# A decode step of attention and feed-forward: wo in one ring buffer, w1 and w2 in another, w2 by block-diagonal columns of h

## The chip, the cores and the metric

The kernel runs on one core of a Trainium2 chip. The metric is the device time of one execution in microseconds (us), median over several runs; lower is better. The engines are named as the profile names them: PE is TensorE's matmuls, PEld its weight loads, DVE is VectorE, ACT ScalarE, SP the engine that issues the loads. "PEclk" is the granted TensorE clock as a share of full speed. A difference counts as faster or slower from 2% on.

## The reference

One token of 512 numbers passes a conditioned layernorm, attention of 32 query heads in 8 groups over 32768 cached positions, an output projection `wo`, a second conditioned layernorm, and a feed-forward of width 1792 with ReLU. Cut to what matters:

```python
h = _layernorm(x) * (1 + ca) + sa
x = x + ga * _A_ref(h, k_cache, v_cache, wq, wo)   # k_cache, v_cache: (1, 8, 32768, 128)
h = _layernorm(x) * (1 + cb) + sb
x = x + gb * (jnp.maximum(h @ w1, 0) @ w2)         # w1: (512, 1792), w2: (1792, 512)
return x                                           # (1, 1, 512), bfloat16
```

The K and V caches are 134 of the 149 MB that have to be read. Everything is used once.

## The kernel before

All large inputs pass through a ring of four buffers of 4 MB in one order on one queue. A transfer is issued when its buffer is free. The end of that order, and the pieces of wo and w2 (cut):

```python
WOP = [(0, Hkv // 2), (Hkv // 2, Hkv // 4), (3 * Hkv // 4, Hkv // 4)]
W2P = [(0, FA - 3), (FA - 3, 2), (FA - 1, 1)]
...
stream += [("v", LAST, (0, 1)), ("v", LAST, (2,)), ("wo", 0), ("v", LAST, (3,)), ("wo", 1), ("wo", 2)]
stream += [("w1",)] + [("w2", i) for i in range(len(W2P))]
```

Each of these ten takes a whole buffer of the ring, so most wait until an earlier one has been used up. The last quarter of V of the last head group (`LAST`) is not multiplied like the others, with 512 columns of V moving, but with V as the stationary operand and 4 columns moving, straight into the transposed output `oT_ps`:

```python
def pv(g, us, js=range(16)):
    ...
    if g == LAST and us[0] == NTILE - 1:
        for j in range(TK):                                   # 64
            c0 = REP * (4 + j // 16)
            nc.tensor.matmul(oT_ps, lhsT=Vs[0][:, j, :], rhs=PT_g[:, j % 16, c0:c0 + REP], start=False, ...)
        return
    ...
            for j in js:                                      # 16 for each quarter
                step(u, V, PTf[:, c0:c0 + 16], V[:, :, Dh * j:Dh * (j + 1)])
```

w2 is applied with one column of h as the stationary operand; the four quarters of the 512 outputs go to partitions 0, 32, 64 and 96, that is to four column groups of the array:

```python
for i in range(KT):                                           # 4
    nc.tensor.matmul(
        ffn_ps[32 * i:32 * i + 1, :], lhsT=hidT[:, ft:ft + 1],
        rhs=w2_sb[:, a, b, i * P:(i + 1) * P], start=False, stop=(ft == FT - 1), skip_group_check=True)
...
nc.scalar.dma_start(out=out[0, 0].rearrange("(i n) -> i n", i=KT),
                    in_=o_bf[:].rearrange("(i r) n -> i r n", r=32)[:, 0, :])
```

Of the kernel before, what the change touches and what calls it, by code (L numbers as in the profile page):

```python
# [9 lines left out]
BF16 = mybir.dt.bfloat16  # L10
F32 = mybir.dt.float32
# [6 lines left out]
def kernel(  # L18
# [28 lines left out]
    WOP = [(0, Hkv // 2), (Hkv // 2, Hkv // 4), (3 * Hkv // 4, Hkv // 4)]  # L47
# [4 lines left out]
    W2P = [(0, FA - 3), (FA - 3, 2), (FA - 1, 1)]  # L52
# [35 lines left out]

    def load(key):
        kind = key[0]  # L90
        if kind == "wm":
            t = ring.tile([P, KT, 6 * D], BF16, tag="slot", name="wm_sb")
            src = wm_v
        elif kind == "wq":
            t = ring.tile([P, KT, Hq * Dh], BF16, tag="slot", name="wq_sb")
            src = wq_v
        elif kind in "kv":
            g, steps = key[1], key[2]
            t = ring.tile([P, TK * len(steps), Dh], BF16, tag="slot", name="Ksb" if kind == "k" else "Vsb")
            src = (kv if kind == "k" else vv)[g, :, TK * steps[0]:TK * (steps[-1] + 1), :]  # L100
        elif kind == "wo":
            t = ring.tile([P, WOP[key[1]][1] * REP, D], BF16, tag="slot", name="wo_sb")
            src = wo_v(key[1])
        elif kind == "w1":
            t = ring.tile([P, KT, Dff], BF16, tag="slot", name="w1_sb")
            src = w1_v
        else:
            a0, n = W2P[key[1]]
            t = ring.tile([P, n, FB, D], BF16, tag="slot", name="w2_sb")
            src = w2_v[:, a0:a0 + n]  # L110
        stream_dma(t[:], src)
        if kind in "kv":
            for i, u in enumerate(steps):
                loaded[(kind, g, u)] = t[:, TK * i:TK * (i + 1), :]
        else:
            loaded[key] = t[:]
# [13 lines left out]
    stream += [("v", LAST, (0, 1)), ("v", LAST, (2,)), ("wo", 0), ("v", LAST, (3,)), ("wo", 1), ("wo", 2)]  # L130
    stream += [("w1",)] + [("w2", i) for i in range(len(W2P))]
# [38 lines left out]
    for n in sorted({n * REP for _, n in WOP}):  # L170
# [20 lines left out]

    rowsel = const.tile([P, 4], F32)
    nc.vector.tensor_copy(out=rowsel[:], in_=ident_f[:].rearrange("p (j c) -> p j c", c=32)[:, :, 0])
# [4 lines left out]
    rowpick = const.tile([P, P], F32)  # L198
    nc.gpsimd.memset(rowpick[:], 0.0)
    nc.vector.tensor_reduce(  # L200
        out=rowpick[:].rearrange("p (j m) -> p j m", m=32)[:, :, 0],
        in_=ident_f[:].rearrange("p (j m) -> p j m", m=32), op=ALU.add, axis=AX.X,
    )
    rowsum = const.tile([P, 1], F32)
    nc.vector.reduce_sum(out=rowsum[:], in_=rowsel[:], axis=AX.X)

# [35 lines left out]
    def layernorm_T(src_T, stat_in, dst_T, shiftT, nscaleT, tagp):  # L242
# [7 lines left out]
        m = nc.tensor.matmul(stat_ps[:], lhsT=onesD_f[:], rhs=stat_in[:], start=True, stop=True)  # L250
        tc.stamp_issue_order_token(m.ins, "pe_tail")
# [10 lines left out]
        a = nc.scalar.activation(out=std[:], in_=negvar[:], func=ACT.Sqrt, bias=eps_t[:], scale=-1.0)  # L262
        tc.stamp_issue_order_token(a.ins, "act_tail")
# [51 lines left out]
    def rows32(src_T, name):  # L315


        e = const.tile([P, 32, KT], F32, name=f"{name}_exp")
        nc.vector.tensor_tensor(
            out=e[:], in0=src_T.unsqueeze(1).to_broadcast([P, 32, KT]),  # L320
            in1=place32[:].unsqueeze(2).to_broadcast([P, 32, KT]), op=ALU.mult,
        )
        r_ps = bank(f"{name}_ps")[:, 0:P]
        m = nc.tensor.matmul(
            r_ps, lhsT=rowpick[:], rhs=e[:].rearrange("p m kt -> p (m kt)"), start=True, stop=True,
        )
        tc.stamp_issue_order_token(m.ins, "pe_tail")
        rows = const.tile([P, P], F32, name=f"{name}_rows")
        a = nc.scalar.copy(out=rows[:], in_=r_ps)
        tc.stamp_issue_order_token(a.ins, "act_tail")  # L330
        return rows

    gb_rows = rows32(modT_sb[:, 5 * KT:6 * KT], "gb")
# [139 lines left out]
    def pv(g, us, js=range(16)):  # L473
# [4 lines left out]
        if g == LAST and us[0] == NTILE - 1:  # L478

            for j in range(TK):  # L480
                c0 = REP * (4 + j // 16)
                nc.tensor.matmul(  # L482
                    oT_ps, lhsT=Vs[0][:, j, :], rhs=PT_g[:, j % 16, c0:c0 + REP],
                    start=False, stop=(j == TK - 1), skip_group_check=True,
                )
            return
# [27 lines left out]
    def blocks(g):  # L514

        o = o_tiles.pop(g)[:].rearrange("p (s d) -> p s d", s=4)
        Y = spool.tile([16, Dh], F32, tag="Y", name="Y", bufs=1)
        nc.vector.tensor_scalar(out=Y[:], in0=o[:, 0], scalar1=smask[:, 0:1], scalar2=None, op0=ALU.mult)
        for s in range(1, 4):
            nc.vector.scalar_tensor_tensor(  # L520
                out=Y[:], in0=o[:, s], scalar=smask[:, s:s + 1], in1=Y[:], op0=ALU.mult, op1=ALU.add,
            )
        Y_tiles[g] = Y
        if g == LAST:
            nc.vector.memset(oT_ps, 0.0)

    def o_cols(g):
        nc.tensor.matmul(  # L528
            oT_ps, lhsT=Y_tiles.pop(g)[:], rhs=qsel, start=(g < LAST), stop=(g < LAST), skip_group_check=True,
        )  # L530
# [33 lines left out]
    def project(i):  # L564
# [3 lines left out]
        for r in range(n):  # L568
            if i == 0:
                nc.tensor.matmul(  # L570
                    a_rows[0][32 * (r % 4):32 * (r % 4) + 1, :], lhsT=o2_tiles[i][:, r:r + 1],
                    rhs=wo_sb[:, r, :], start=False, stop=(r >= n - 4), skip_group_check=True,
                )
                continue
# [10 lines left out]
    def join_rows():  # L585
        a_sb = rows_sb("a_sb")[:, 0, :]
        nc.scalar.copy(out=a_sb, in_=a_rows[0])
        for ko in range(KT):
            yield
            nc.tensor.matmul(  # L590
                attnT_ps[:, ko:ko + 1], lhsT=a_sb.rearrange("q (m ko) -> q ko m", ko=KT)[:, ko, :],
                rhs=rowsum[:], start=False, stop=False, skip_group_check=True,
            )

    with tc.manual_schedule(engines={mybir.EngineType.PE, mybir.EngineType.DVE}):
# [66 lines left out]
        pv(LAST, (2,))  # L662
        blocks(LAST)
        project(0)
        o_cols(LAST)
        join = join_rows()
        next(join)
        pv(LAST, (3,))
        next(join)
        next(join)  # L670
        normalise(LAST)
        for _ in join:
            pass
        for i in range(1, len(WOP)):
            project(i)


    ffn_ps = bank("ffn_ps")[:, 0:P]
    nc.vector.memset(ffn_ps, 0.0)
    stat2 = const.tile([P, 2], F32)  # L680
    x1T = const.tile([P, KT], F32)
    nc.vector.tensor_tensor(out=x1T[:], in0=attnT_ps, in1=modT_sb[:, 2 * KT:3 * KT], op=ALU.mult)
    nc.vector.scalar_tensor_tensor(
        out=x1T[:], in0=x1T[:], scalar=1.0, in1=xT, op0=ALU.mult, op1=ALU.add, accum_out=stat2[:, 0:1],
    )
    h2T = const.tile([P, KT], BF16)
    layernorm_T(x1T[:], stat2, h2T[:], modT_sb[:, 3 * KT:4 * KT], ncb[:], "ln2")

    x1_rows = rows32(x1T[:], "x1")

    w1_sb = need(("w1",))
    w1_f = w1_sb.rearrange("p kt (a m b) -> p kt a b m", m=P, b=FB)
    hidT_ps = small_ps([P, FT], "hidT_ps")
    for ft in range(FT):
        for kt in range(KT):
            nc.tensor.matmul(
                hidT_ps[:, ft:ft + 1], lhsT=w1_f[:, kt, ft // FB, ft % FB, :], rhs=h2T[:, kt:kt + 1],
                start=(kt == 0), stop=(kt == KT - 1),
            )
    hidT = const.tile([P, FT], BF16)  # L700
    nc.scalar.activation(out=hidT[:], in_=hidT_ps[:], func=ACT.Relu)
    for part, (base, n) in enumerate(W2P):
        w2_sb = need(("w2", part))
        for a in range(n):
            for b in range(FB):
                ft = (base + a) * FB + b
                for i in range(KT):
                    nc.tensor.matmul(  # L708
                        ffn_ps[32 * i:32 * i + 1, :], lhsT=hidT[:, ft:ft + 1],
                        rhs=w2_sb[:, a, b, i * P:(i + 1) * P], start=False, stop=(ft == FT - 1),  # L710
                        skip_group_check=True,
                    )
    o_rows = const.tile([P, P], F32)
    nc.vector.tensor_tensor(out=o_rows[:], in0=ffn_ps, in1=gb_rows[:], op=ALU.mult)  # L714
    o_bf = const.tile([P, P], BF16)
    nc.vector.tensor_tensor(out=o_bf[:], in0=o_rows[:], in1=x1_rows[:], op=ALU.add)  # L716
    nc.scalar.dma_start(
        out=out[0, 0].rearrange("(i n) -> i n", i=KT),
        in_=o_bf[:].rearrange("(i r) n -> i r n", r=32)[:, 0, :],
    )  # L720
# [30 lines left out]
```

## Time and profile before

356.12 us is the median of 6 runs (355.97 to 356.60).

| | before |
|---|---|
| span of the profiled run | 354.3 us |
| busy share PE, DVE, ACT | 78%, 58%, 8% |
| share of the load queue's packets | 98.2% |
| last K tile landed | 302.89 us |
| last quarter of V landed | 336.83 us |
| x1T (the input of the second layernorm) begins | 343.40 us |
| w2's matmuls | 348.6 to 350.9 us |

The busy shares say little, since the stages differ. The end is what decides: which of the last waits is for a transfer, and which for an engine. The prediction shows those views. Two more lines serve for comparison, from the views of single tiles of the kernel before; the three numbers after the colon are the shortest, median and longest duration in ns, then come first and last start:

```profile
L708 PE MATMUL ffn_ps<-w_sb,hidT x56: 264/311/315, 348.6 to 350.6; 128*1 128x128 bf16 x56
L717 ACTq DMA_DIRECT2D out_dram<-o_bf x1: 1098/1098/1098, 351.6 to 351.6; - x1
```

A single w2 matmul lasts 311 ns, yet 56 of them start within 2 us, with two waits for data among them: they overlap. The issue of the 1 KB output takes 1.1 us.

### The profile page before, as it was taken

How to read it: one execution, taken by the hardware profiler on the slowest of the kernel's cores; microseconds unless marked ns; L12 is line 12 of the kernel's file. 1: busy time of each engine (PE TensorE's matmuls, PEld its weight loads, DVE VectorE, ACT ScalarE, POOL GpSimd, SP SyncE). 2: the span in 40 equal slices, each digit the busy share in tenths (PEclk: the TensorE clock that was granted, in tenths of full speed). 3: DMA queues.
4: the chain of work that ended last, by engine and by line, in shares of the span. 5: the costliest groups of instructions: out<-in, count | busy, mean ns of one | idle time of the engine just before them, and what ended most of it. 6: DMA issues, size and time to landing. Idle time of an engine off the chain costs nothing. (4 is left out here: it accounts for less than half of the span.)

```text
span 354.3 us, 4169 instructions
## 1 busy us (share of the span) xinstructions
PE 276.4 (78%) x1403; PEld 114.0 (32%) x1403; DVE 205.8 (58%) x266; ACT 28.9 (8%) x70; POOL 8.4 (2%) x14
## 2 busy tenths in 40 slices
PE   0453793799798979897979796989789787989884
PEld 0121231233233323332333233333333233333373
DVE  8537683973848366571949177553938095843221
ACT  1023004000110011001100101010100010010110
POOL 9000000000000000000000000000000000000000
PEclk9966867699899999999999998899999999999955
DMA  8999999999999999999999999999999999999994
GB/s 313 449 422 455 420 426 451 422 429 425 446 429 414 459 425 416 459 422 422 455 422 425 442 433 426 436 436 422 425 451 425 422 453 425 422 455 403 424 418 164
DMA packets 6613, 149.61 MB, mean 422 GB/s; under 512 B 712, under 2 KB 712, under 8 KB 1608
## 3 DMA queue, kind: packets, MB, share of 16 engines
q1 hardware_dynamic: 6592, 149.43, 98.2%
q8 instruction: 9, 0.15, 0.1%
q14 instruction: 4, 0.03, 0.0%
q10 hardware_dynamic: 8, 0.00, 0.0%
HBM read 149.42 MB, written 0.00 MB: 422 GB/s over the span
## 5 line engine op out<-in xcount | busy, mean ns | idle before, releaser
L398 DVE STREAM_TRANSPOSE KTt<-Ksb 128x2048 f32<-128x2048 f32 x64 | 143.3, 2283 | 61.9 <-DMA Ksb<-in_A_k_cache_dram 52.6
L489 PE MATMUL o_ps<-Vsb,PT_g 128*16 (+1 forms) x496 | 124.9, 387 | 23.4 <-ACT qbd L382 7.8
L418 PE MATMUL S_ps<-KTt,qbd 128*128 128x512 bf16 x512 | 124.1, 395 | 17.9 <-DVE KTt L398 16.2
L418 PEld LDWEIGHTS <-qbd 128*128 128x128 bf16 x512 | 50.0, 100 | 83.3 <-issue 27.4
L489 PEld LDWEIGHTS o_ps<-Vsb,PT_g 128*16 x416 | 36.4, 87 | 90.9 <-issue 66.4
L424 DVE TENSOR_SCALAR_CACHE_REDUCE S_g<-S_ps 128x512 f32<-128x512 f32 x16 | 11.1, 691 | 29.2 <-PE S_ps L418 29.2
L382 ACT COPY qbd<-qrep_sb 32x128 bf16<-32x128 bf16 x32 | 9.4, 295 | 137.1 <-PE S_ps L418 136.0
L461 DVE STREAM_TRANSPOSE PT_g<-P_g 128x1024 bf16<-128x1024 bf16 x8 | 9.7, 1218 | 6.5 <-ACT P_g L455 6.5
L452 ACT ACTIVATE nbias<-Mb_ps 128x1 f32<-128x1 f32 x8 | 1.4, 171 | 130.8 <-PE Mb_ps L450 130.8
L489 PEld LDWEIGHTS <-PT_g 128*16 128x16 bf16 x80 | 6.9, 90 | 10.1 <-issue 0.8
L219 PE MATMUL xc_ps<-cx_sel,cx_bd 16*128 16x2 bf16 x4 | 0.3, 172 | 12.1 <-DVE cx_bd L213 12.1
L455 ACT ACTIVATE P_g<-S_g,nbias 128x1024 bf16<-128x1024 f32 x8 | 9.2, 1149 | 0.2
L520 DVE SCALAR_TENSOR_TENSOR Y<-o_ps,smask,Y 16x128 f32<-16x128 f32 x24 | 8.0, 335 | 0.8
L159 DVE COPY sel<-ident_bf 128x128 bf16<-128x128 bf16 x4 | 7.5, 3688 | 0.0
L541 DVE TENSOR_TENSOR oT_sb<-acc_ps,Linv 128x4 bf16<-128x4 f32 x8 | 1.2, 151 | 9.4 <-PE acc_ps L528 5.6
L467 PE MATMUL L_ps<-Lexp,ones_f 128*128 128x4 f32 x16 | 3.0, 258 | 4.3 <-DVE Lexp L464 4.3
L439 DVE TENSOR_REDUCE Mrow<-mT_ps 1x4 f32<-1x128 f32 x8 | 2.1, 257 | 6.9 <-PE mT_ps L436 6.9
L355 PE MATMUL q_ps<-wq_sb,hT 128*1 128x512 bf16 x32 | 3.6, 625 | 3.0 <-DVE hT L270 3.0
L436 PE MATMUL mT_ps<-ident_f,m_p 128*1 128x128 f32 x8 | 2.2, 270 | 3.9 <-DVE m_p L433 2.0
L467 PEld LDWEIGHTS L_ps<-Lexp,ones_f 128*128 128x128 f32 x16 | 3.1, 222 | 5.7 <-issue 5.1
L287 PE MATMUL mod_ps<-wm_sb,siluT 128*1 128x512 bf16 x24 | 3.4, 612 | 1.2 <-DVE siluT L281 1.2
L510 DVE MEMSET o_ps<- 16x512 f32 x8 | 3.9, 485 | 0.8
(115 smaller groups left out, 84.4 us busy)
## 6 DMA issues: line engine op xcount, KB each, us to landing
Ksb<-in_A_k_cache_dram SPq DMA_DIRECT2D x16, 4096.0 KB, 29.8
Vsb<-in_A_v_cache_dram SPq DMA_DIRECT2D x15, 4096.0 KB, 24.2
wq_sb<-in_A_wq_dram SPq DMA_DIRECT2D x1, 4096.0 KB, 18.7
Vsb<-in_A_v_cache_dram SPq DMA_DIRECT2D x2, 2048.0 KB, 17.9
wm_sb<-in_w_mod_dram SPq DMA_DIRECT2D x1, 3072.0 KB, 10.3
wo_sb<-in_A_wo_dram SPq DMA_DIRECT2D x1, 2048.0 KB
wo_sb<-in_A_wo_dram SPq DMA_DIRECT2D x2, 1024.0 KB, 8.0
w_sb<-in_B_w_dram SPq DMA_DIRECT2D x1, 1792.0 KB, 10.7
```

Of the source, the lines that this page charges most:

```text
L159: nc.vector.tensor_copy(out=sel[:, hp, :].rearrange("p (a c) -> p a c", a=4), in_=src)
L355: nc.tensor.matmul(q_ps[i][32 * a:32 * a + 1, :].rearrange("o (h e) -> o h e", e=32), lhsT=hT[:, kt:kt + 1], rhs=wq_f[:, kt, i, a], start= ...
L382: nc.scalar.copy(out=o, in_=i)
L398: t = nc.vector.transpose(out=KTt[:].bitcast(F32), in_=Ksb[:, 32 * half:32 * half + 32, :].rearrange("p j d -> p (j d)").bitcast(F32),)
L418: nc.tensor.matmul(S_ps_tiles[g], lhsT=qbd[g % 2][:, hp, s, :], rhs=KTv[:, 16 * sl:16 * sl + 16, h, :, par], start=(t4 == 0 and sl == 0 an ...
L424: nc.vector.tensor_scalar(out=S_tiles[g][:, G, :], in0=S_ps_tiles[g], scalar1=1.0, scalar2=None, op0=ALU.mult, op1=ALU.max, accum_out=m_ti ...
L455: nc.scalar.activation(out=P_g[:], in_=S_g[:].rearrange("p g f -> p (g f)"), func=ACT.Exp, bias=nbias[:], scale=scale, accum_out=l_g[:],)
L461: nc.vector.transpose(out=PT_g[:], in_=P_g[:])
L467: nc.tensor.matmul(L_ps[:], lhsT=ones_f[:], rhs=Lexp[:], start=True, stop=True)
L489: nc.tensor.matmul(o_tiles[g][:], lhsT=PT, rhs=Vx, start=False, stop=False, skip_group_check=True)
L510: nc.vector.memset(o_tiles[g][:], 0.0)
L520: nc.vector.scalar_tensor_tensor(out=Y[:], in0=o[:, s], scalar=smask[:, s:s + 1], in1=Y[:], op0=ALU.mult, op1=ALU.add,)
```

## The change

The intent: with the last two quarters of V in one buffer, all of wo in a second and w1 with w2 in a third, every load can be issued early. V then comes ahead of wo, and fewer bytes and less work stand behind the last landing. The rows of wo's product are turned by VectorE instead of being picked out by matmuls of full width; for that, `project` reads the rows of wo and writes their product in another order (`"p (a m ko) -> p a ko m"`, not in the cut). Spare matmuls are put in to hold the clock; w2 accumulates into four adjacent partitions, so that the last two VectorE instructions and the output touch 4 partitions. Cut to the core:

```diff
-    WOP = [(0, Hkv // 2), (Hkv // 2, Hkv // 4), (3 * Hkv // 4, Hkv // 4)]
+    WOP = [(0, Hkv // 2), (Hkv // 2, Hkv // 4), (Hkv - 2, 1), (Hkv - 1, 1)]
-    W2P = [(0, FA - 3), (FA - 3, 2), (FA - 1, 1)]
+    W2P = [(0, 2, slice(0, FB)), (2, FA - 5, slice(0, FB)), (FA - 3, 1, slice(0, FB)), (FA - 2, 1, slice(0, FB)),
+           (FA - 1, 1, slice(0, 1)), (FA - 1, 1, slice(1, FB))]
+    W1P = [(0, KT - 1), (KT - 1, KT)]
...
+    def piece(name, at, n):
+        if name not in pieces:
+            pieces[name] = ring.tile([P, 2 * TK * Dh], BF16, tag="slot", name=name)
+        return pieces[name][:, at:at + n]
...
-    stream += [("v", LAST, (0, 1)), ("v", LAST, (2,)), ("wo", 0), ("v", LAST, (3,)), ("wo", 1), ("wo", 2)]
+    stream += [("v", LAST, (0, 1)), ("v", LAST, (2,)), ("v", LAST, (3,))] + [("wo", i) for i in range(len(WOP))]
...
-        if g == LAST and us[0] == NTILE - 1:          # the 64 small matmuls
-            ...
-            return
...
     def join_rows():
-        a_sb = rows_sb("a_sb")[:, 0, :]
-        nc.scalar.copy(out=a_sb, in_=a_rows[0])
+        aT = rows_sb("aT")[:, 0, :]
+        nc.vector.transpose(out=aT, in_=a_rows[0])
...
+    def keep_clock(n):
+        for _ in range(n):
+            nc.tensor.matmul(spare[0], lhsT=ident_bf[:], rhs=qbd[0][:, 0, 0:4, :], start=True, stop=True)
...
         pv(LAST, (2,))
+        pv(LAST, (3,))
         blocks(LAST)
         project(0)
+        keep_clock(2)
         o_cols(LAST)
+        keep_clock(2)
         normalise(LAST)
+        project(1)
+        keep_clock(3)
+        project(2)
+        join_rows()
+        keep_clock(4)
+        project(3)
...                                                    # 4 before and 4 after the layernorm statistics,
...                                                    # 1 after each of two rows of w1, 1 after w1
-                        ffn_ps[32 * i:32 * i + 1, :], lhsT=hidT[:, ft:ft + 1],
+                        ffn_ps, lhsT=hid_bd[:, ft, i, :],      # 4 columns, h in the i-th, zeros in the others
...
-        in_=o_bf[:].rearrange("(i r) n -> i r n", r=32)[:, 0, :],
+    nc.scalar.dma_start(out=out[0, 0].rearrange("(i n) -> i n", i=KT), in_=o_bf[:])
```

More of the change, by code (lines that the diff above doesn't have):

```diff
@@ L45 @@
     NG = NTILE // 2
-    WOP = [(0, Hkv // 2), (Hkv // 2, Hkv // 4), (3 * Hkv // 4, Hkv // 4)]
+    WOP = [(0, Hkv // 2), (Hkv // 2, Hkv // 4), (Hkv - 2, 1), (Hkv - 1, 1)]
+    WOROWS = 2
     LAST = Hkv - 1
@@ L87 @@
     loaded, last_loop = {}, []
+    pieces = {}
+    def piece(name, at, n):
+        if name not in pieces:
+            pieces[name] = ring.tile([P, 2 * TK * Dh], BF16, tag="slot", name=name)
+        return pieces[name][:, at:at + n]
     def load(key):
@@ L98, in load @@
             g, steps = key[1], key[2]
-            t = ring.tile([P, TK * len(steps), Dh], BF16, tag="slot", name="Ksb" if kind == "k" else "Vsb")
             src = (kv if kind == "k" else vv)[g, :, TK * steps[0]:TK * (steps[-1] + 1), :]
+            name = "Ksb" if kind == "k" else "Vsb"
+            if len(steps) == 2:
+                t = ring.tile([P, TK * len(steps), Dh], BF16, tag="slot", name=name)
+            else:
+                t = piece(name, TK * Dh * (steps[0] % 2), TK * Dh).rearrange("p (j d) -> p j d", d=Dh)
         elif kind == "wo":
-            t = ring.tile([P, WOP[key[1]][1] * REP, D], BF16, tag="slot", name="wo_sb")
+            g0, n = WOP[key[1]]
+            t = piece("wo_sb", g0 * REP * D, n * REP * D).rearrange("p (r d) -> p r d", d=D)
             src = wo_v(key[1])
         elif kind == "w1":
-            t = ring.tile([P, KT, Dff], BF16, tag="slot", name="w1_sb")
-            src = w1_v
-        else:
-            a0, n = W2P[key[1]]
-            t = ring.tile([P, n, FB, D], BF16, tag="slot", name="w2_sb")
-            src = w2_v[:, a0:a0 + n]
+            k0, k1 = W1P[key[1]]
+            t = piece("w12_sb", k0 * Dff, (k1 - k0) * Dff).rearrange("p (kt f) -> p kt f", f=Dff)
+            src = w1_v[:, k0:k1]
+        else:
+            a0, n, bs = W2P[key[1]]
+            nb = bs.stop - bs.start
+            t = piece("w12_sb", KT * Dff + (a0 * FB + bs.start) * D, n * nb * D)
+            t = t.rearrange("p (a b d) -> p a b d", a=n, b=nb)
+            src = w2_v[:, a0:a0 + n, bs]
         stream_dma(t[:], src)
@@ L129 @@
             stream += [(kind, gg, (2 * G, 2 * G + 1)) for kind, gg in (("k", g + 1), ("v", g))]
-    stream += [("v", LAST, (0, 1)), ("v", LAST, (2,)), ("wo", 0), ("v", LAST, (3,)), ("wo", 1), ("wo", 2)]
-    stream += [("w1",)] + [("w2", i) for i in range(len(W2P))]
+    stream += [("v", LAST, (0, 1)), ("v", LAST, (2,)), ("v", LAST, (3,))] + [("wo", i) for i in range(len(WOP))]
+    stream += [("w1", i) for i in range(len(W1P))] + [("w2", i) for i in range(len(W2P))]
     pos = [0]
@@ L188 @@
     oA = [const.tile([P, n * REP, P // (n * REP)], BF16, name=f"oA{i}") for i, (_, n) in enumerate(WOP)]
-    rowsel = const.tile([P, 4], F32)
-    nc.vector.tensor_copy(out=rowsel[:], in_=ident_f[:].rearrange("p (j c) -> p j c", c=32)[:, :, 0])
     place32 = const.tile([P, 32], F32)
@@ L197 @@
     )
-    rowpick = const.tile([P, P], F32)
-    nc.gpsimd.memset(rowpick[:], 0.0)
+    rowpick = const.tile([P, KT], F32)
     nc.vector.tensor_reduce(
-        out=rowpick[:].rearrange("p (j m) -> p j m", m=32)[:, :, 0],
-        in_=ident_f[:].rearrange("p (j m) -> p j m", m=32), op=ALU.add, axis=AX.X,
-    )
-    rowsum = const.tile([P, 1], F32)
-    nc.vector.reduce_sum(out=rowsum[:], in_=rowsel[:], axis=AX.X)
+        out=rowpick[:], in_=ident_f[:].rearrange("p (j m) -> p j m", m=32), op=ALU.add, axis=AX.X,
+    )
+    hid_bd = const.tile([P, FT, KT, KT], BF16)
+    nc.gpsimd.memset(hid_bd[:], 0.0)
     pick8 = const.tile([16, 8], BF16)
@@ L249, in layernorm_T @@
         stat_ps = small_ps([P, 2], f"stat_ps_{tagp}")
-        m = nc.tensor.matmul(stat_ps[:], lhsT=onesD_f[:], rhs=stat_in[:], start=True, stop=True)
-        tc.stamp_issue_order_token(m.ins, "pe_tail")
+        nc.tensor.matmul(stat_ps[:], lhsT=onesD_f[:], rhs=stat_in[:], start=True, stop=True)
         nu = const.tile([P, KT], F32, name=f"nu_{tagp}")
@@ L261, in layernorm_T @@
         std = const.tile([P, 1], F32, name=f"std_{tagp}")
-        a = nc.scalar.activation(out=std[:], in_=negvar[:], func=ACT.Sqrt, bias=eps_t[:], scale=-1.0)
-        tc.stamp_issue_order_token(a.ins, "act_tail")
+        nc.scalar.activation(out=std[:], in_=negvar[:], func=ACT.Sqrt, bias=eps_t[:], scale=-1.0)
         cen = const.tile([P, KT], F32, name=f"cen_{tagp}")
@@ L313, with four_rows @@
         )
-    def rows32(src_T, name):
+    def four_rows(src_T, name, copy):
         e = const.tile([P, 32, KT], F32, name=f"{name}_exp")
@@ L322, in rows32 @@
         )
-        r_ps = bank(f"{name}_ps")[:, 0:P]
-        m = nc.tensor.matmul(
+        r_ps = bank(f"{name}_ps")[0:KT, 0:P]
+        nc.tensor.matmul(
             r_ps, lhsT=rowpick[:], rhs=e[:].rearrange("p m kt -> p (m kt)"), start=True, stop=True,
         )
-        tc.stamp_issue_order_token(m.ins, "pe_tail")
-        rows = const.tile([P, P], F32, name=f"{name}_rows")
-        a = nc.scalar.copy(out=rows[:], in_=r_ps)
-        tc.stamp_issue_order_token(a.ins, "act_tail")
+        rows = const.tile([KT, P], F32, name=f"{name}_rows")
+        copy(out=rows[:], in_=r_ps)
         return rows
-    gb_rows = rows32(modT_sb[:, 5 * KT:6 * KT], "gb")
+    gb_rows = four_rows(modT_sb[:, 5 * KT:6 * KT], "gb", nc.scalar.copy)
     hT = const.tile([P, KT], BF16)
@@ L477, in pv @@
         Vs = [need(("v", g, u)) for u in us]
-        if g == LAST and us[0] == NTILE - 1:
-            for j in range(TK):
-                c0 = REP * (4 + j // 16)
-                nc.tensor.matmul(
-                    oT_ps, lhsT=Vs[0][:, j, :], rhs=PT_g[:, j % 16, c0:c0 + REP],
-                    start=False, stop=(j == TK - 1), skip_group_check=True,
-                )
-            return
         def step(u, V, PT, Vx):
@@ L523, in blocks @@
         Y_tiles[g] = Y
-        if g == LAST:
-            nc.vector.memset(oT_ps, 0.0)
     def o_cols(g):
         nc.tensor.matmul(
-            oT_ps, lhsT=Y_tiles.pop(g)[:], rhs=qsel, start=(g < LAST), stop=(g < LAST), skip_group_check=True,
+            oT_ps, lhsT=Y_tiles.pop(g)[:], rhs=qsel, start=True, stop=True, skip_group_check=True,
         )
@@ L568, in project @@
         for r in range(n):
-            if i == 0:
+            if i < WOROWS:
                 nc.tensor.matmul(
-                    a_rows[0][32 * (r % 4):32 * (r % 4) + 1, :], lhsT=o2_tiles[i][:, r:r + 1],
-                    rhs=wo_sb[:, r, :], start=False, stop=(r >= n - 4), skip_group_check=True,
+                    a_rows[0][32 * (r % 4):32 * (r % 4) + 1, :].rearrange("o (a ko m) -> o a ko m", a=4, ko=KT), lhsT=o2_tiles[i][:, r:r + 1],
+                    rhs=wo_sb[:, r, :].rearrange("p (a m ko) -> p a ko m", a=4, ko=KT), start=False, stop=(i == WOROWS - 1 and r >= n - 4), skip_group_check=True,
                 )
@@ L585, in join_rows @@
     def join_rows():
-        a_sb = rows_sb("a_sb")[:, 0, :]
-        nc.scalar.copy(out=a_sb, in_=a_rows[0])
-        for ko in range(KT):
-            yield
+        aT = rows_sb("aT")[:, 0, :]
+        nc.vector.transpose(out=aT, in_=a_rows[0])
+        for a in range(4):
             nc.tensor.matmul(
-                attnT_ps[:, ko:ko + 1], lhsT=a_sb.rearrange("q (m ko) -> q ko m", ko=KT)[:, ko, :],
-                rhs=rowsum[:], start=False, stop=False, skip_group_check=True,
-            )
+                attnT_ps[32 * a:32 * a + 32, :], lhsT=place32[:],
+                rhs=aT.rearrange("p (a ko m) -> p a ko m", a=4, ko=KT)[:, a, :, 0],
+                start=False, stop=False, skip_group_check=True,
+            )
+    spare = []
+    def keep_clock(n):
+        if not spare:
+            spare.append(bank("spare_ps"))
+        for _ in range(n):
+            nc.tensor.matmul(spare[0], lhsT=ident_bf[:], rhs=qbd[0][:, 0, 0:4, :], start=True, stop=True)
     with tc.manual_schedule(engines={mybir.EngineType.PE, mybir.EngineType.DVE}):
@@ L662 @@
         pv(LAST, (2,))
+        pv(LAST, (3,))
         blocks(LAST)
         project(0)
+        keep_clock(2)
         o_cols(LAST)
-        join = join_rows()
-        next(join)
-        pv(LAST, (3,))
-        next(join)
-        next(join)
-        normalise(LAST)
-        for _ in join:
-            pass
-        for i in range(1, len(WOP)):
-            project(i)
-    ffn_ps = bank("ffn_ps")[:, 0:P]
-    nc.vector.memset(ffn_ps, 0.0)
-    stat2 = const.tile([P, 2], F32)
-    x1T = const.tile([P, KT], F32)
@@ L682 @@
-    nc.vector.tensor_tensor(out=x1T[:], in0=attnT_ps, in1=modT_sb[:, 2 * KT:3 * KT], op=ALU.mult)
-    nc.vector.scalar_tensor_tensor(
-        out=x1T[:], in0=x1T[:], scalar=1.0, in1=xT, op0=ALU.mult, op1=ALU.add, accum_out=stat2[:, 0:1],
-    )
-    h2T = const.tile([P, KT], BF16)
-    layernorm_T(x1T[:], stat2, h2T[:], modT_sb[:, 3 * KT:4 * KT], ncb[:], "ln2")
-    x1_rows = rows32(x1T[:], "x1")
-    w1_sb = need(("w1",))
-    w1_f = w1_sb.rearrange("p kt (a m b) -> p kt a b m", m=P, b=FB)
-    hidT_ps = small_ps([P, FT], "hidT_ps")
@@ L694 @@
-    for ft in range(FT):
-        for kt in range(KT):
-            nc.tensor.matmul(
-                hidT_ps[:, ft:ft + 1], lhsT=w1_f[:, kt, ft // FB, ft % FB, :], rhs=h2T[:, kt:kt + 1],
-                start=(kt == 0), stop=(kt == KT - 1),
-            )
-    hidT = const.tile([P, FT], BF16)
-    nc.scalar.activation(out=hidT[:], in_=hidT_ps[:], func=ACT.Relu)
-    for part, (base, n) in enumerate(W2P):
-        w2_sb = need(("w2", part))
-        for a in range(n):
-            for b in range(FB):
-                ft = (base + a) * FB + b
-                for i in range(KT):
+        keep_clock(2)
@@ new lines @@
+        normalise(LAST)
+        project(1)
[4 more added lines that the diff above has]
+        project(3)
+        hidT_ps = small_ps([P, FT], "hidT_ps")
+        nc.vector.memset(hidT_ps[:], 0.0)
+        stat2 = const.tile([P, 2], F32)
+        x1T = const.tile([P, KT], F32)
+        nc.vector.tensor_tensor(out=x1T[:], in0=attnT_ps, in1=modT_sb[:, 2 * KT:3 * KT], op=ALU.mult)
+        nc.vector.scalar_tensor_tensor(
+            out=x1T[:], in0=x1T[:], scalar=1.0, in1=xT, op0=ALU.mult, op1=ALU.add, accum_out=stat2[:, 0:1],
+        )
@@ L708 @@
+        h2T = const.tile([P, KT], BF16)
+        keep_clock(4)
+        layernorm_T(x1T[:], stat2, h2T[:], modT_sb[:, 3 * KT:4 * KT], ncb[:], "ln2")
+        keep_clock(4)
+        for part, (k0, k1) in enumerate(W1P):
+            w1_f = need(("w1", part)).rearrange("p kt (a m b) -> p kt a b m", m=P, b=FB)
+            for kt in range(k0, k1):
+                for ft in range(FT):
                     nc.tensor.matmul(
-                        ffn_ps[32 * i:32 * i + 1, :], lhsT=hidT[:, ft:ft + 1],
@@ L710 @@
-                        rhs=w2_sb[:, a, b, i * P:(i + 1) * P], start=False, stop=(ft == FT - 1),
-                        skip_group_check=True,
-                    )
-    o_rows = const.tile([P, P], F32)
-    nc.vector.tensor_tensor(out=o_rows[:], in0=ffn_ps, in1=gb_rows[:], op=ALU.mult)
-    o_bf = const.tile([P, P], BF16)
-    nc.vector.tensor_tensor(out=o_bf[:], in0=o_rows[:], in1=x1_rows[:], op=ALU.add)
-    nc.scalar.dma_start(
-        out=out[0, 0].rearrange("(i n) -> i n", i=KT),
-        in_=o_bf[:].rearrange("(i r) n -> i r n", r=32)[:, 0, :],
-    )
+                        hidT_ps[:, ft:ft + 1], lhsT=w1_f[:, kt - k0, ft // FB, ft % FB, :], rhs=h2T[:, kt:kt + 1],
@@ new lines @@
+                        start=False, stop=(kt == KT - 1), skip_group_check=True,
+                    )
+                if kt < KT - 2:
+                    keep_clock(1)
+        hb = hid_bd[:]
+        nc.scalar.activation(
+            out=AP(hb.tensor, hb.offset, [hb.ap[0], [KT * KT, FT], [KT + 1, KT]]),
+            in_=hidT_ps[:].unsqueeze(2).to_broadcast([P, FT, KT]), func=ACT.Relu,
+        )
+        x1_rows = four_rows(x1T[:], "x1", nc.vector.tensor_copy)
+        keep_clock(1)
+        ffn_ps = bank("ffn_ps")[0:KT, 0:P]
@@ new lines @@
+        last = len(W2P) - 1
+        for part, (base, n, bs) in enumerate(W2P):
+            w2_sb = need(("w2", part))
+            for a in range(n):
+                for b in range(bs.start, bs.stop):
+                    ft = (base + a) * FB + b
+                    for i in range(KT):
+                        nc.tensor.matmul(
+                            ffn_ps, lhsT=hid_bd[:, ft, i, :], rhs=w2_sb[:, a, b - bs.start, i * P:(i + 1) * P],
+                            start=(part == 0 and a == 0 and b == 0 and i == 0), stop=(ft == FT - 1 and i == KT - 1),
+                        )
@@ L724 @@
+        o_rows = const.tile([KT, P], F32)
+        nc.vector.tensor_tensor(out=o_rows[:], in0=ffn_ps, in1=gb_rows[:], op=ALU.mult)
+        o_bf = const.tile([KT, P], BF16)
+        nc.vector.tensor_tensor(out=o_bf[:], in0=o_rows[:], in1=x1_rows[:], op=ALU.add)
+    nc.scalar.dma_start(out=out[0, 0].rearrange("(i n) -> i n", i=KT), in_=o_bf[:])
 _INS = ['A_x', 'A_k_cache', 'A_v_cache', 'A_wq', 'A_wo', 'B_x', 'B_w1', 'B_w2', 'c', 'w_mod']
```

## The prediction

> **What bounds the kernel now.** I read the page's DMA part first. One queue carries all the input, and its packets fill 98.2% of the span on the 16 engines.
>
> ```profile
> q1 hardware_dynamic: 6592, 149.43, 98.2%
> HBM read 149.42 MB, written 0.00 MB: 422 GB/s over the span
> PEclk9966867699899999999999998899999999999955
> ```
>
> 98.2% of 354.3 us is 347.9 us, and the change moves the same 149.43 MB. What is left to win is the start, which is not touched, and the end. So nothing near 2% (7 us) is there to be won, and everything is decided after the last K tile has landed at 302.9 us. The last row says that the TensorE clock is at half in the last two slices.
>
> Second, the chain that ended last, in order of time, shows what the end hangs on:
>
> ```profile
> 302.89 0.02 issue
> ...
> 316.55 5.71 PE o_ps L489 x26
> ...
> 322.29 14.55 DMA Vsb<-in_A_v_cache_dram
> ...
> 336.88 1.81 PE acc_ps L482 x64
> 338.69 0.95 PE acc_ps L590 x4
> ...
> 342.32 7.49 DMA w_sb<-in_B_w_dram
> ...
> 351.31 0.29 DVE o_bf L716
> ```
>
> The reader should see two transfers in it: the last quarter of V of the last head group, which is issued only at 322.29 because its buffer is not free before, and the last piece of w2. Between them stands a chain of small work that ends just in time.
>
> Third, the timeline of the tail shows how much slack that chain has:
>
> ```profile
> 323.42 7.07 PE L489 MATMUL o_ps<-Vsb,PT_g 128*16 128x512 bf16 x32 [0.85 <-DVE o_ps L510]
> ...
> 330.73 3.19 PE L489 MATMUL o_ps<-Vsb,PT_g 128*16 128x512 bf16 x14
> ...
> 343.40 0.16 DVE L682 TENSOR_TENSOR x1T<-acc_ps,modT_sb 128x4 f32<-128x4 f32 x1 [2.86 <-PE acc_ps L576]
> ...
> 345.62 0.22 DVE L270 SCALAR_TENSOR_TENSOR h2T<-cen_ln,rstd_ln,modT_sb 128x4 bf16<-128x4 f32 x1
> ...
> 346.05 1.65 PE L696 MATMUL hidT_ps<-h2T,w_sb 128*128 128x1 bf16 x56 [0.81 <-DMA w_sb<-in_B_w_dram]
> ...
> 348.60 1.02 PE L708 MATMUL ffn_ps<-w_sb,hidT 128*1 128x128 bf16 x32 [0.89 <-DMA w_sb<-in_B_w_dram]
> ```
>
> h2T is ready at 345.84 and w1 is there at 346.05: 0.2 us of slack. The w2 work could begin at 348.0 and waits until 348.6 for its data: 0.6 us of slack. A tail that is later by more than about 0.8 us is no longer hidden by the transfers. After the w2 work (350.92) come two VectorE instructions, the issue of the output (1.10 us from 351.64) and its landing: 3.4 us to the end.
>
> The windows of the tail give the clock and the DMA:
>
> ```profile
> 334.00:336.00 2.00, 1.24 (x16) 0.35 (x11) 1.41 (x5) 0.71 (x2) 0.00 (x0) 1.00 0.93 393
> 336.00:338.00 2.00, 1.47 (x46) 1.38 (x47) 0.00 (x0) 1.16 (x1) 0.00 (x0) 0.91 1.00 422
> 338.00:340.00 2.00, 1.62 (x30) 1.53 (x27) 0.31 (x2) 0.00 (x0) 0.00 (x0) 0.50 1.07 454
> ```
>
> The last three columns are granted clock, DMA share and GB/s. PE idles around 335 to 336.9, waiting for V, and soon the clock is 0.50 and stays there. DMA is full throughout, so the late issue of that V piece costs no bandwidth; it only decides the order in which bytes come.
>
> **What the Trainium skill says.** "TensorE: Matmul & The Clock Gate", Part 1 (the HAM clock gate), has two clocks, 1.2 and 2.4 GHz, and an activity window of about 3.4 us, an idle one giving the half clock. The windows above agree with 1.00 and 0.50. The same page, section "Back-to-back issue gap", puts matmuls of 128 columns at about 56 ns apart warm and 107 ns cold, and at about 81 ns in a stream with weight loads. The trace has no such stream; for 512 columns it shows 7.07 us for 32, 0.22 us each, which fits 213 ns at full clock. "TensorEngine Tiling (Array Packing)", "Available Configurations", says that stationary tiles of 32 columns run four at a time. The trace agrees: the 32 matmuls of w2 took 1.02 us at half clock, 32 ns each, well under 107. "DMA: Bandwidth & Descriptors", "Specifications", gives a fabric ceiling of 435 GB/s; the trace has 422 as a mean, so the stream can't be made faster to speak of.
>
> **The change part by part.**
>
> Transfers. V's last quarter shares a buffer with the third and is issued before wo. wo0's 2.10 MB no longer stand before it: at about 0.425 MB/us that is 4.9 us, so it lands near 331.9 instead of 336.83. wo, w1 and w2 end at the same byte of the stream as before: wo near 341.7, w1 near 346.0, the last of w2 near 350.4. The three quarters of w1 that come first land about 1 us sooner. w2 now ends in two pieces of 128 KB with rows of 1 KB; only 4 matmuls wait for the last one, instead of 8. Alone, this is worth about 0.2 us at the end.
>
> PE, from the end of the first half of V at 330.42. Spreading head group 6 is now PE work of its own and stands in front of the next V: it waits for two VectorE instructions (0.16 and 0.23 us), so V goes on near 331.3 instead of 330.73. Two quarters of V as 32 matmuls of 0.215 us are 6.9 us: to 338.2. Before, the last quarter was 64 small ones of 27 ns, 1.8 us; it now takes 3.4, so what the earlier landing gave is spent here. Then the masked sums on VectorE (0.34 + 1.08 us): to 339.9. Beside them project(0) (16 at about 0.1 us, the spacing of the rows of wo before) and two spare matmuls: PE free at 340.2. Turning the columns 0.4, normalising 0.4, spread 0.2, 8 rows of wo 0.8: to 342.0. Three spare ones (0.65) and 16 small ones (0.45): 343.1, with the VectorE turn of the rows beside them (128x2048 took 2.27 us, so 128x512 about 0.57). Join, about 0.4 as estimated (before it was 2.1 us at half clock with 128 stationary columns, now 32), four spare (0.86), 16 small (0.45) and their latency (0.17): x1T can start at about 344.95, against 343.40 before.
>
> Layernorm, 2.4 us as before: h2T at 347.35, now 1.3 us after w1. 56 matmuls of w1 at 27 ns plus two spare ones and latency, 2.1 us; Relu 0.2: 349.65. Then w2: 56 matmuls of 128 columns that all write the same four partitions, so the fourfold overlap is gone: 56 x 56 ns is 3.1 us at full clock, plus 0.2 latency: 352.95, against 350.92. This is the disputed place: PE, not the last transfer, would set the end. The two VectorE instructions keep their 128 elements per partition, so 0.29 us each. The output from adjacent partitions may be issued faster than in 1.10 us; I count nothing for it.
>
> Sum: 352.95 - 350.92 = +2.0 us, so 358.1 by this count. The spare matmuls, 22 in all at 0.215 us (4.7 us of PE), are partly on this path; what they buy is the full clock for w2, worth 56 x 51 ns = 2.9 us.
>
> **The rivals.** First: the end stays with the transfers, w2 keeps up, and only the shorter finish counts. The places of the spare matmuls speak for it: they look as if PE had time to fill there. Against it speaks that PE is busy without a gap from 314.9 to 334.1 and I see no gap after it. The time would be 355 to 356. Second: the clock falls all the same, in the layernorm (2.4 us with some 2 us of PE work in it) or in w1, whose matmuls move one column each; it fell before in the midst of small matmuls. Then w2 takes 6.0 us: about 361. Third: w2 runs at the spacing of 81 ns that the page gives with weight loads: 4.5 us, about 359.5. Fourth: the output is issued in some 0.4 us, as the small loads on the other queue are (0.37): 0.7 us less in any case.
>
> **Range and chances.** The count says 358.1. I move it down to 357.3, because the fourth rival and a faster join or row work pull down, and because whoever placed the spare matmuls may have seen slack that I don't. Low end 354.9: first rival with a cheaper output. High end 360.4: half of the second rival or all of the third. 2% is 7.1 us: below 349.0 is out of reach of a stream of 347.9 us plus a 2 us start and a 3 us finish; above 363.2 needs the half clock and more. So faster 0.01, same 0.96, slower 0.03.
>
> **What would show each step.** In the changed kernel: DMA share about 1.0 until 349 or so and the same last landing; V's last quarter landed by 332; x1T at 344 to 345.5; granted clock near 1.00 in the last 15 us; PE working through the 56 w2 matmuls with no wait for w2 data and ending after 352; the chain going through PE from about 315 to the end rather than through a w transfer. If w2's matmuls wait for their transfers to the last piece, my central step is wrong and the first rival right. If the clock is 0.5, the second. The prediction fails outright if the stream itself gets faster or slower, which I have no cause to expect.

## The result and the profile after

The changed kernel took 359.18 us, median of 6 runs (358.39 to 360.26), against 356.12. The ratio is 1.0085, 95% interval 1.0065 to 1.0106. Ratios here are the mean time of one kernel's fast runs over the mean of the other's in the same rounds, so not quite the ratio of the medians; in the later experiments the traced run is left out of them. It is a loss of 3.1 us, small but clear of noise.

The page of the changed kernel has these lines in answer to the first ones of the prediction:

```profile
q1 hardware_dynamic: 7056, 149.43, 97.3%
PEclk9996996799899999999969999999999896999999
```

The same bytes take the same time: 97.3% of 358.0 us is 348.3 us, against 347.9. Its clock row ends in nines instead of fives, so the spare matmuls do what they are for. It also has dips before that, one near 300 us.

The chain that ended last (start, duration, what) no longer contains a transfer after 307.6 us:

```profile
324.42 7.07 PE o_ps L489 x32
...
332.56 6.57 PE o_ps L489 x30
...
343.99 0.75 PE spare_ps L601 x3
...
345.43 0.97 PE spare_ps L601 x4
346.39 0.51 PE acc_ps L574 x16
...
351.77 3.30 PE ffn_ps L724 x56
355.08 0.02 issue
355.10 0.29 DVE o_rows L729
```

From 316 us on it is PE but for short steps of VectorE and ScalarE, none over 0.50 us, and spare matmuls are among its links. The windows of that trace (the last three columns are clock, DMA share and GB/s) show that the data had come before:

```profile
348.00:350.00 2.00, 1.60 (x27) 0.93 (x26) 1.09 (x6) 0.29 (x1) 0.00 (x0) 1.00 0.54 197
350.00:352.00 2.00, 1.75 (x48) 1.41 (x47) 0.28 (x1) 0.29 (x1) 0.00 (x0) 1.00 0.00 1
352.00:354.00 2.00, 2.00 (x39) 2.00 (x37) 0.00 (x0) 0.00 (x0) 0.00 (x0) 1.00 0.00 0
```

The last piece of w2 landed near 350.4 (issued at 341.6, 8.8 us to landing), as it did in the kernel before (343.4 and 7.1); w2's matmuls begin 1.4 us later. The two tiles of before, now:

```profile
L724 PE MATMUL ffn_ps<-w_sb,hid_bd x56: 218/219/220, 351.8 to 354.8; 128*4 128x128 bf16 x56
L732 ACTq DMA_DIRECT2D out_dram<-o_bf x1: 551/551/551, 355.7 to 355.7; - x1
```

One w2 matmul is shorter (219 ns, full clock), but 56 of them now take 3.29 us, since they start one after the other, 56 ns apart. The output is issued in 0.55 us instead of 1.10: the only part of the change that shows as a gain at the end.

**A second trace.** The changed kernel was traced once more, with three rounds:

> The changed kernel once more, for its spread and a second trace. If the fall of the clock near 296 to 302 us, which its first trace has and that of the last-V-small run has not, is a chance of the run: runs in two groups about 1 us apart, some at 358.4 and some at 359.5. If the kernel brings it on each time: one group at 359.2.

It took 359.00 us (358.35 to 359.62), ratio 1.009 (1.0075 to 1.0105); the traced run 358.65. The windows around 300 us, first of the first trace, then of this one:

```profile
296.00:300.00 4.00, 3.29 (x11) 1.47 (x10) 0.97 (x5) 0.00 (x0) 0.00 (x0) 0.50 0.99 426
```

```profile
296.00:300.00 4.00, 3.20 (x17) 1.38 (x15) 1.02 (x5) 0.00 (x0) 0.00 (x0) 1.00 0.97 418
```

In the first trace the clock is at half there and fewer matmuls are done (11 against 17); the V of the last head group begins at 324.42. In the second it begins at 323.29 (before: 323.42). So a fall of the clock long before the tail goes with 1.1 us at the end in this pair of traces. Some of the 10 runs of this kernel lie near 358.4 and some near 359.5, as a chance event would make them, though they don't fall into two clean groups. For the working below the second trace is the one to compare with before: its span is 356.9, 2.6 us more than 354.3.

### The profile page after: what moved, and what is told of

Same layout as the page of the kernel before. It is cut to its first block, busy times and chain, and to the rows that moved or that the text cites. A ratio compares the mean times of both kernels' runs of the same rounds, so it can differ in the third digit from the quotient of the medians.

```text
span 358.0 us, 4070 instructions
## 1 busy us (share of the span) xinstructions
PE 281.7 (79%) x1351; PEld 114.3 (32%) x1354; DVE 207.7 (58%) x269; ACT 28.2 (8%) x68; POOL 8.5 (2%) x14
## 3 DMA queue, kind: packets, MB, share of 16 engines
q1 hardware_dynamic: 7056, 149.43, 97.3%
## 5 line engine op out<-in xcount | busy, mean ns | idle before, releaser
L489 PE MATMUL o_ps<-Vsb,PT_g 128*16 (+1 forms) x512 | 129.5, 393 | 22.4 <-ACT qbd L391 9.7
L427 PEld LDWEIGHTS <-qbd 128*128 128x128 bf16 x512 | 49.0, 98 | 86.4 <-issue 28.6
L489 PEld LDWEIGHTS o_ps<-Vsb,PT_g 128*16 x416 | 37.2, 89 | 90.2 <-issue 63.9
L489 PEld LDWEIGHTS <-PT_g 128*16 128x16 bf16 x96 | 8.4, 90 | 12.1 <-issue 0.8
L518 DVE TENSOR_SCALAR Y<-o_ps,smask 16x128 f32<-16x128 f32 x8 | 2.2, 271 | 6.8 <-PE o_ps L489 6.8
L601 PE MATMUL spare_ps<-qbd,ident_bf 128*128 128x512 bf16 x19 | 5.4, 380 | 0.2 <-issue 0.2
```

The source lines that it names most:

```text
L427: nc.tensor.matmul(S_ps_tiles[g], lhsT=qbd[g % 2][:, hp, s, :], rhs=KTv[:, 16 * sl:16 * sl + 16, h, :, par], start=(t4 == 0 and sl == 0 an ...
L489: nc.tensor.matmul(o_tiles[g][:], lhsT=PT, rhs=Vx, start=False, stop=False, skip_group_check=True)
L601: nc.tensor.matmul(spare[0], lhsT=ident_bf[:], rhs=qbd[0][:, 0, 0:4, :], start=True, stop=True)
```

## The experiments

The theory: after the last K tile PE is the bound, and three parts of the change put work on PE's path: the last quarter of V as 16 wide matmuls instead of 64 small ones, the spare matmuls, and w2 without the overlap of the column groups. Rivals: the transfers or the waits for VectorE set the pace; or the clock does. Each kernel ran beside the kernel before, and all were correct. The kernel before took 355.88 us in the first four experiments and 355.80 in the others, against 356.12 beside the change. So what a run gains or loses against the change is taken from how far each stands above the kernel before in its own rounds; for the change that is 3.1 us. The traces give a second figure, the difference of their spans, if a trace with the fall of the clock near 296 us is set against the first trace of the change and one without it against the second.

**Spare matmuls doubled.** `for _ in range(n)` in `keep_clock` became `for _ in range(2 * n)`.

> The changed kernel with every run of spare matmuls doubled (44 instead of 22). Theory one, PE alone sets the end from the last scores on: of the 22 added ones of 0.215 us (4.7 us) nearly all lie on the path, so 363 to 364 us against 359.2 for the change. Rival, PE has idle time between these steps and the transfers or VectorE set the pace: under 1 us more, 359 to 360.

363.12 us, ratio 1.0199 (1.0186 to 1.0212): 4.2 us more than the change (3.9 by the traces, 361.9 against 358.0), for 22 matmuls of 0.215 us, 4.7 us in sum. Most of an addition to PE goes straight into the time. The rival of idle time falls.

**No spare matmuls.** `keep_clock` does nothing.

> The changed kernel without the spare matmuls. From its trace some 2.4 us of the 4.7 are on the path, the rest lies in waits for VectorE. Theory one, the clock stays at 1.00 without them: 356.8 us. Theory two, they are needed: the clock falls to 0.5 in layernorm or w1, w2 takes 6 us instead of 3.3, and the time is 359 to 360.5, no gain. The granted clock of the windows from 345 us on tells which.

358.16 us, ratio 1.0067 (1.0053 to 1.0081): 0.8 us less than the change (0.6 by the traces, 357.4 against 358.0), neither of the two sizes expected, because both effects occur. The layernorm begins at 345.02 instead of 346.94 and w2 at 349.40 instead of 351.77, but the clock falls, as the windows show:

```profile
346.00:348.00 2.00, 0.71 (x27) 0.68 (x26) 1.10 (x6) 0.30 (x1) 0.00 (x0) 0.58 1.07 409
348.00:350.00 2.00, 2.00 (x45) 1.56 (x43) 0.28 (x1) 0.30 (x1) 0.00 (x0) 0.50 0.59 206
350.00:352.00 2.00, 2.00 (x21) 2.00 (x20) 0.00 (x0) 0.00 (x0) 0.00 (x0) 0.50 0.00 0
```

w2 then takes 5.05 us instead of 3.29. The spare matmuls buy 1.8 us in w2 and cost 2.4 on the way there. The exchange is shown; the net loss of 0.6 to 0.8 us where they stand is not clear of noise, since the intervals of the two ratios overlap (1.0053 to 1.0081 here, 1.0065 to 1.0106 for the change).

**w2 in four column groups again.** In the changed kernel:

```diff
-                            ffn_ps, lhsT=hid_bd[:, ft, i, :], ...
+                            ffn_ps[32 * i:32 * i + 1, :], lhsT=hidT[:, ft:ft + 1], ...
```

with the gate and x1 in rows at partitions 0, 32, 64, 96, and the output from there.

> The changed kernel with w2 as before: the four quarters of a row in four column groups, output from partitions 0, 32, 64, 96. If losing the overlap of the column groups is a main cause: the 56 matmuls of w2 take 1.4 to 1.9 us instead of 3.3, the issue of the output goes back from 0.55 to 1.1 us, 358.0 in all, 1.1 less than the change. If PE is not the bound there: no less, or 0.5 more.

357.32 us, ratio 1.0040 (1.0027 to 1.0053): 1.6 us less than the change (1.6 by the traces too, 356.4 against 358.0), though the output's issue is back at 1.10 us. The tile's view shows why it is more than expected:

```profile
L737 PE MATMUL ffn_ps<-w_sb,hidT x56: 217/219/219, 352.0 to 352.7; 128*1 128x128 bf16 x56
```

All 56 start within 0.73 us, 13 ns apart on average, where the block-diagonal ones are 56 ns apart. What the narrower output saves (0.55 us) is a quarter of what the lost overlap costs (3.29 less 0.95, 2.3 us).

**The last quarter of V small again.** The branch with 64 small matmuls is put back into `pv`, `oT_ps` is zeroed after `normalise(LAST - 1)`, and the last `o_cols` adds to it.

> The changed kernel with the last quarter of V as 64 small matmuls straight into the column of the output, as before. If PE sets the end all the way from 323 us: 1.7 us off PE work (3.44 less 1.73) and 1.7 us off the time, 357.5. If the wait is elsewhere (wo pieces, VectorE): less than 0.7 us.

357.24 us, ratio 1.0046 (1.0032 to 1.0061): 1.7 us less than the change, as expected (1.4 by the traces, 355.5 against 356.9). In its trace the 64 take 1.75 us.

**The transfers alone.** The kernel before, with the buffers, pieces and order of the change, and the last quarter of V multiplied, still as 64 small ones, ahead of the first part of wo:

```diff
-        blocks(LAST)
-        project(0)
-        o_cols(LAST)
-        join = join_rows()
-        next(join)
-        pv(LAST, (3,))
+        blocks(LAST)
+        pv(LAST, (3,))
+        o_cols(LAST)
+        project(0)
+        join = join_rows()
```

> The kernel before with the transfers of the change (last V quarter ahead of wo, one buffer for wo, one for w1 and w2, w1 in two pieces and w2 in six), and nothing of its arithmetic: the last V quarter stays 64 small matmuls, now in front of project(0), w2 in four column groups, no spare matmuls. Theory: V lands near 332, the gap of PE at 335 to 337 goes, x1T comes 1 us or more earlier, and w2 waits for its last piece all the same: 355.6 to 356.1, no gain over 355.9. Rival, V's landing was what held the end: 354.5 or less.

355.86 us, ratio 1.0004 (0.9991 to 1.0017): no gain and no loss. The V quarter is taken up at 333.88 instead of 336.88 and is done before the first wo piece, but the gap has only moved: PE now waits for that piece until 336.47, the clock falls as before, and x1T begins at 343.27, so the 1 us expected there was not won. The end of the chain is again a transfer:

```profile
341.31 8.83 DMA w_sb<-in_B_w_dram
350.14 0.04 issue
350.19 0.30 PE ffn_ps L725 x4
```

**The w2 part alone.** The kernel before with block-diagonal columns and adjacent outputs, no spare matmuls.

> The kernel before with only the w2 part of the change: block-diagonal columns, four adjacent output partitions. Its clock is 0.5 there, so 56 matmuls of 128 columns at about 107 ns take 6 us from 348.0 or 348.6 on, against an end at 350.9: 3.7 later, the output issued 0.55 us faster, about 359. If the clock rises in the midst of them, about 358. If PE kept up with the transfers: 355.4.

358.19 us, ratio 1.0068 (1.0055 to 1.0081): 2.4 us lost by this part alone. The 56 matmuls run from 348.48 for 4.91 us; the clock is 0.50 until about 352 and rises only then. That is the second of the three expectations. It also shows that early transfers and V have no share in this part of the loss.

**Three parts undone.** The changed kernel with the small V, w2 in column groups and no spare matmuls. What stays is the transfers, the pieces of wo, and the turning of its rows by VectorE.

> The changed kernel with three of its parts undone: last V quarter small, w2 in column groups, no spare matmuls. If these three are all of the loss, PE is ahead of the transfers again and w2 waits for its last piece: 355.5 to 356.2, the time of the kernel before, whatever the clock does. If the turning of the wo rows by VectorE or the extra spread cost something too: above 356.5.

355.97 us, ratio 1.0005 (0.9992 to 1.0018): the time of the kernel before, within its noise, at half clock from 342 us on. The three parts are the whole loss; the rest of the change costs nothing in the time and wins nothing, since the last w2 piece is waited for again (PE's last 16 matmuls at 349.76, after a wait for the transfer). Undone one by one the three give 0.8, 1.6 and 1.7 us, 4.1 in sum (3.6 by the traces); together they give only about 3, after which the transfers are the bound again. In the changed kernel the new order of wo's rows also lies on PE's path (see the part on the prediction); it was not undone alone.

**Is there a version that beats both?** The adjacent output is worth 0.55 us, if PE can be early enough to do w2 at full clock behind its transfers. First with 10 spare matmuls, in places where the trace of the change seems to wait:

> The changed kernel with the last V quarter small and with the spare matmuls only where PE waits anyway (two fours around the layernorm statistics, one after each of the first two rows of w1): 10 instead of 22. Theory: x1T near 342.5, w2 can begin near 347 at full clock, keeps up with its transfers, and the shorter output issue is a gain: 355.0 to 355.4, about 0.2% under the kernel before. If the clock falls in w1 or w2: 357 to 358.

356.37 us, ratio 1.0011 (0.9997 to 1.0025), in two groups: three runs at 355.5 to 355.8, three at 356.9. The traced run is of the second, with the clock at 0.50 near 296 us. The clock also fell at 342 to 346, and there the four spare matmuls ahead of the layernorm statistics took 1.87 us and held it up. Then with 11, placed by these traces:

> As the run before it with 10 spare matmuls, but 11 of them placed only where that run's trace or the one without any shows PE idle: two behind the last columns, one before the third piece of wo, two before the layernorm statistics, five behind them, one behind w1; none between the rows of w1. Theory: the clock stays at 1.00 from 340 us on, w2 begins near 347.2 and runs 3.3 us to 350.5, only just behind its transfers: 355.0 to 355.4 in runs without a fall of the clock near 296 us, about 356 in runs with one. If the clock still falls before w2: 357 or more.

355.53 us (355.25 to 356.96), ratio 0.9998 (0.9984 to 1.0012). In the trace the clock is 1.00 from 340 us to the end of w2, w2 begins at 347.11 and ends at 350.5, and the span is 353.5, 0.8 us under before. Five of six runs lie at 355.25 to 355.70, one at 356.96. The median is under both kernels, but the interval holds 1: a gain over the kernel before is not shown, only one over the change.

## Why the prediction was right

The measured 359.18 lies in the range of 354.9 to 360.4 and within 2%, as said. The mechanism was the central one, PE and not the last transfer setting the end; 357.3 was 1.9 us too low. By its steps:

- **The stream is unchanged and full.** Right: 149.43 MB, and 348.3 us of packets against 347.9; the last quarter of V landed near 331.8 (issued at 308.0, 23.8 us to landing), counted 331.9. V's earlier landing gave nothing, as the run with the transfers alone shows.
- **V resumes near 331.3 and is done near 338.2.** Right in the second trace: 331.36 and, with the last wide matmul begun at about 338.2, 338.4. What early V gave was spent on wide matmuls; undoing that gives 1.7 us, with 1.6 counted (3.4 for 1.8).
- **The stretch from there to x1T** was mis-sized. Counted 344.95, measured 345.81. The whole 0.86 us is there when the 8 rows of wo's second part end, at 342.86 where 342.0 was counted. The 16 first rows and their two spare matmuls end at 340.79 instead of 340.2: the rows come 0.15 us apart where 0.1 was taken from before (13 in 2.19 us, 0.38 of it the last one's own length). The 8 rows take 1.00 us instead of 0.8. What the count left out is the new order in which these rows are read and written. The tile's view, of the kernel before and of the change, shows how long one row takes:

```profile
L570 PE MATMUL a_ps<-wo_sb,o_sb x16: 377/377/379, 333.5 to 334.8; 128*1 128x512 bf16 x16
```

```profile
L568 PE MATMUL a_ps<-wo_sb,o_sb x24: 609/630/642, 338.8 to 343.4; 128*1 128x512 bf16 x24
```

Both are at full clock. Sixteen rows in a run take 1.25 us in the old order (the run with the transfers alone) and 2.01 in the new (three parts undone). Whether the reading or the writing is slow was not separated. VectorE turns the rows in 0.72 us, not 0.57, but here nothing waits for it: it is done at 343.63, and the join comes behind 16 small matmuls at 344.05. The join takes 0.17 us instead of 0.4, which makes up for spare and small matmuls that take a little longer than counted.

- **x1T to the start of w2** was counted 4.7 us and measured 4.83: the spare matmul after w1, which the count left out, is in it.
- **w2 at 56 ns each, with no overlap, 3.3 us.** Right to the digit: 3.29. The rival spacing of 81 ns did not appear.
- **The end of w2** was counted 352.95; it is 353.97 undisturbed, 355.10 in the first trace. The difference of the two is the fall of the clock near 300 us, which no step had. In the kernel before, most of such a fall would be hidden by the waits for V until 336.88 and for w1 and w2; that is argued, since no trace of it has one. Here nothing hides it. The spread agrees: in its four sets of runs the kernel before stayed within 0.4 to 0.8 us, in its two the change within 1.3 and 1.9.
- **The rivals.** The first, end set by transfers, is refuted by the chain and by doubling the spare matmuls. The guess behind it, that whoever placed these had seen slack, was one of the reasons to move the figure down by 0.8 us from 358.1, which was the wrong direction. The point held against it was misread in part: PE was not busy without a gap from 314.9 to 334.1, since the prediction's own line at 323.42 has a wait of 0.85 us before it. Another reading is off without effect: the transfer of w2 in the chain is the second of its three pieces, which 16 matmuls wait for; the last landed near 350.4. The half clock did not come, because of the spare matmuls: without them it does. The fourth rival was right: the output is issued in 0.55 us, 0.55 less, counted as nothing.

What made the prediction low is thus the downward move and the under-sized stretch before x1T (0.86 us, some 0.7 of it rows of wo), with the missed dip on top and the output's gain against it: 358.1 + 0.86 + 0.13 - 0.55 is 358.5, and the undisturbed traced run took 358.65. The output's gain, counted as nothing, hid part of the miss; that it is no larger is luck to that extent. What stays open is why the clock falls near 296 us in some runs: it is in five of the eight traces of kernels that keep most of the changed tail (in a sixth it falls for a shorter time), and in none of the traces of the kernel before, of its two variants and of the one with three parts undone. The five traced runs with the full fall are the slowest or among the slower of their kernel's runs, and the three without it or with the shorter one among the faster, so it goes with the spread of these kernels. Whether it comes from the kernel or from chance, twelve traces don't settle.

## What to carry to other kernels

When a kernel is bound by its transfers, first measure how much slack each engine has in front of the last of them; a rearrangement of the tail is free only inside that slack, and here it was 0.2 us before w1 and another 0.6 us before w2. Four outputs side by side are cheaper to store than four spread over column groups, but they give up the groups' overlap; weigh 0.55 us of output against 2.3 us of matmuls. Spare matmuls that hold the clock belong only where the trace shows PE waiting: on the path 22 more of them, 4.7 us of PE, cost 3.9 to 4.2 us. An order of operands that spares another engine work can cost PE: here 0.63 us for a row of wo instead of 0.38.

## What the Trainium skill lacked or had wrong

- "TensorE: Matmul & The Clock Gate", section "Back-to-back issue gap": it puts sustained streams of weight load and matmul at about 81 ns for 128 columns and 131 ns for 512. The runs show 56 ns for 128 columns with 4-column weights loaded each time (56 in 3.29 us) and 0.22 us for 512, with 16-column weights (32 in 7.07 us) and with 128-column ones (32 in 7.14 us).
- The same page, Part 1 (the HAM clock gate), ties the fall of the clock to an idle window, in one case to frequent short idle times between groups of matmuls, and does not say how small matmuls count. In the run with three parts undone the clock fell while PE counted as busy for 1.42 and 1.79 us of 2.00; the work there was rows of wo (one stationary column, 512 moving) and matmuls of 1 to 4 moving columns, with waits of up to 0.6 us. Which of these let it fall is not shown:

```profile
338.00:340.00 2.00, 1.42 (x15) 0.49 (x11) 0.61 (x3) 0.00 (x0) 0.00 (x0) 1.00 1.05 434
340.00:342.00 2.00, 1.79 (x37) 0.97 (x30) 0.79 (x2) 0.00 (x0) 0.00 (x0) 0.90 1.04 429
342.00:344.00 2.00, 1.12 (x18) 0.95 (x16) 0.74 (x7) 0.00 (x0) 0.00 (x0) 0.50 0.95 395
```

- None of the pages searched says that the issue of a small store depends on its partitions: 1.10 us from partitions 0, 32, 64 and 96, 0.55 us from four adjacent ones, for the same 1 KB.
